# Two layers of an expert in one loop: four accumulators held open, and weight pieces fetched three steps before they are split

## The chip, the core and the metric

The kernel runs on one core of a Trainium2 chip. TensorE (PE) multiplies, VectorE (DVE), ScalarE (ACT) and GpSimd (POOL) work on tiles in on-chip memory, SyncE (SP) issues most of the transfers, ACT and POOL issue some. Each engine takes its instructions strictly in the order in which they stand, and an instruction that waits holds back all that stand behind it on that engine. The metric is the device time of one execution in microseconds (us); less is better.

## What is computed

Three stages follow each other on 4608 tokens of 512 features, in float32. The change lies in the second, so that stands here in full, and the others in a line or two:

```python
# 1: retention (8 batches, 8 heads, 576 positions, 64 features a head): x, 4608 x 512
ret = (scale * q @ k.T) * Dmat ; x = ret @ v
# 2: a layer of 8 experts; each token goes to the expert with the largest logit
expert_idx = argmax(normed(x) @ normed(expert_emb).T / tau)
for e in range(8):
    mask = expert_idx == e
    h = maximum(x[mask] @ w1[e], 0.0)          # 512 -> 1024
    out[mask] = gate_w[mask, None] * (h @ w2[e])   # 1024 -> 512
# 3: a dense layer, weights given in float64 by their bits
h = x @ w_in ; g = h * cos(h) ; y = g @ w_out  # 512 -> 2048 -> 512
```

## The kernel before

Every float32 product is done as three matmuls on operands split into a high and a low part (`mm3`, L84 to L87: high by high, high by low, low by high). The split of a weight is two instructions: ACT rounds the fetched piece to the high part (L190), POOL subtracts to get the low part (L191). `fetch_piece` (L176) issues the transfer of a piece of 128 x 1024 values on SP into one of three staging buffers (`st`), `split_piece` (L184) makes the split; `load_piece` does one right behind the other.

Stage 1 scatters each token's row to a region of its expert in a table in memory. Stage 2 takes the experts in order of their size; each expert's tokens are cut into two blocks ("halves", 16 in all, of 312 down to 272 columns by `HCS`). For a block:

- `load_half` brings the token rows (tile `nat`), `rows_to_x` turns them by twelve PE transposes (tile `xt`) and ACT and DVE split them (tile `x`, L267, L268).
- `layer1` runs over eight groups f of 128 hidden features: twelve matmuls into one bank of PSUM (tile `h`), then ACT takes relu into the high part of `hs` (L286) and DVE the low part (L287). All eight `hs` are kept.
- `layer2` runs over four groups d of 128 output features: for each, 24 matmuls over all eight `hs` into one bank (tile `y`), a DVE copy (L308), and a transfer of the result to a buffer in memory, `x2t[d]` (L309).

So all of `layer1` of a block stands ahead of its transposes for the next block, and these ahead of `layer2`. The pieces of the next expert's weights are loaded beside: the four of w1 when the expert's first block begins, the four of w2 in the second block after every other f. From the fourth block on, `decode64` turns 32 pieces of the float64 weights of stage 3 into float32, in the same staging buffers: seven instructions on ACT, DVE and POOL and a transfer back to memory (`wf`). At the first block of the first expert stands an `If` for experts with more tokens than two blocks hold; with this input its body isn't run.

Stage 3 (`load_x2`, `ffn1_mm`, `ffn2`) reads `x2t` back, 512 columns at a time and one d after the other, splits it (tile `xf`, L825, L826) and alternates the matmuls of the first layer (tile `f`) with those of the second, which go into four accumulators held open (tile `o`). It begins with six groups of `f` that go over d in the outer loop.

The order in which each engine's instructions stand is made by a scheduler from the order of the code, its dependencies and its own estimates of time; `tc.issue_after(x)` forces an instruction behind x on its engine. PSUM has eight banks, and every `bank(...)` takes a free one and waits for the readers of the last tile in it.

Of the kernel before, what the change touches and what calls it, by code (L numbers as in the profile page):

```python
# [36 lines left out]
DECODE_AT = ((0, 2, 4), (0, 2))  # L37
# [12 lines left out]
PAD = 2  # L50
PIECE_AT = ((3, 2), (3, 4), (4, 0), (5, 2), (5, 4), (6, 0))
# [3 lines left out]
def retention_moe_ffn(  # L55
# [116 lines left out]

    wcount = [0]
    wpools = {"a": wa}

    def fetch_piece(src, a, nm):  # L176
        st = stage.tile([P, 1024], F32, tag="st", name=f"st{nm}")
        nc.sync.dma_start(st.rearrange("p (a b) -> p a b", a=a) if a > 1 else st, src)
        return st
# [17 lines left out]
    def w2_src(e, i):  # L197
        return w2[ds(e, 1), :, i * P : (i + 1) * P].rearrange("o (c p) d -> p (o c) d", p=P)

    def w1_piece(e, i):  # L200
        return load_piece(w1_src(expert[e], i), 4)

    def w2_piece(e, i):
        return load_piece(w2_src(expert[e], i), 8)

    def win_piece(i):
        return load_piece(wf32[i], 1)
# [8 lines left out]
    def decode64(n):  # L216
        i, c = n // 2, n % 2
        st = stage.tile([P, 1024], F32, tag="st", name=f"sd{n}")
        if i < 8:
            src = w_in32[c * 256 : (c + 1) * 256, i * 512 : (i + 1) * 512].rearrange("(c p) f -> p c f", p=P)  # L220
            nc.sync.dma_start(st.bitcast(I32).rearrange("p (a b) -> p a b", a=2), src)
        else:
            nc.sync.dma_start(st.bitcast(I32), w_out32[(n - 16) * P : (n - 15) * P, :])
# [4 lines left out]
        tb = mp["dec"].tile([P, 512], F32, tag="tb", name=f"tb{n}")  # L228
        nc.scalar.activation(ta, hi_f, AF.Abs)
        nc.vector.scalar_tensor_tensor(hi_f, ta, TINY64, hi_f, op0=ALU.is_ge, op1=ALU.mult)  # L230
# [6 lines left out]
        nc.vector.tensor_scalar(tb.bitcast(I32), lo_w, 9, None, op0=ALU.logical_shift_right)  # L237
# [4 lines left out]
        nc.sync.dma_start(wf32[i][:, c * 512 : (c + 1) * 512], ta)  # L242
# [3 lines left out]
    def load_rows(row0, nm, pool, hc):  # L246
# [3 lines left out]
        for ins in (i1, i2):  # L250
            after_all("xs", ins)
        return t

    def copy_ids(row0, col0, hc):
        ins = nc.sync.dma_start(idl[ds(col0, hc), :], xs_d[ds(row0, hc), DM : DM + 1])
        after_all("xs", ins)

    def rows_to_x(t, nm, pool, hc):
        x = pool.tile([P, 2, NP, hc], F32R, tag="x", name=f"x_{nm}")
        for c in range(3):  # L260
            n = P if c < 2 else hc - 256
            ps = bank(f"xt{c}_{nm}")
            for d in range(NP):
                nc.tensor.transpose(ps[:, d * n : (d + 1) * n], t[:n, c, d * P : (d + 1) * P], ident[:n, :n])
            pv = ps[:, : NP * n].rearrange("p (a b) -> p a b", a=NP)
            hi = x[:, 0, :, c * P : c * P + n]
            nc.scalar.copy(hi, pv)  # L267
            nc.vector.tensor_tensor(x[:, 1, :, c * P : c * P + n], pv, hi, op=ALU.subtract)  # L268
        return x

    def layer1(x, wp, nm, hc, after=None):
        hs = []
        for f in range(FE // P):
            ps = bank(f"h{f}_{nm}")
            w = wp(f // 2)
            for c in range(NP):
                o = c * 256 + (f % 2) * P
                mm3(
                    ps[:, :hc],
                    lambda s: w[:, s, o : o + P],  # L280
                    lambda s: x[:, s, c, :],
                    c == 0,
                    c == NP - 1,
                )
            h = mp['h'].tile([P, 2, hc], F32R, tag="h", name=f"hs{f}_{nm}")
            nc.scalar.activation(h[:, 0], ps[:, :hc], AF.Relu)  # L286
            nc.vector.scalar_tensor_tensor(  # L287
                h[:, 1], ps[:, :hc], 0.0, h[:, 0], op0=ALU.max, op1=ALU.subtract
            )
            hs.append(h)  # L290
            if after is not None:
                after(f)
        return hs

    def layer2(hs, wp, nm, col, hc, after=None, queue=None):
        for d in range(NP):
            ps = bank(f"y{d}_{nm}")
            w = wp(d)
            for f in range(FE // P):
                mm3(  # L300
                    ps[:, :hc],
                    lambda s: w[:, s, f * P : (f + 1) * P],
                    lambda s: hs[f][:, s],
                    f == 0,
                    f == FE // P - 1,
                )
            y = mp["y"].tile([P, hc], F32, tag="y", name=f"y{d}_{nm}")
            nc.vector.tensor_copy(y, ps[:, :hc])  # L308
            (queue or nc.sync).dma_start(x2t[d][:, ds(col, hc)], y)  # L309
            if after is not None:  # L310
                after(d)
# [5 lines left out]
    w1p, w2p = {}, {}  # L317
# [6 lines left out]

    def load_half(i):
        e, j = halves[i]
        natt[i] = load_rows(entry(1 + j, e), f"{e}_{j}", natp[i % 3 != 1], HCS[e])
# [3 lines left out]
    with ExitStack() as actx:  # L331
# [282 lines left out]
        for i, (b, c) in enumerate(seq):  # L614
# [8 lines left out]
            if i == len(seq) - 1:  # L623
                x0 = rows_to_x(early["rows"], "0_0", xp[0], HCS[0])
# [12 lines left out]
            if fetched and fetched[0][0] <= i - 2:  # L637
                key, st = fetched.pop(0)[1:]
                with tc.issue_after(state["pool"].ins):
                    (w1p if key < 4 else w2p)[(0, key % 4)] = split_piece(st)  # L640
# [351 lines left out]
```

## Time and profile before

| | us |
|---|---|
| time, median of 3 runs | 1524.63 (1522.89 to 1530.38) |
| the profiled execution: its time, its span | 1515.07, 1511.8 |
| its mean granted TensorE clock, as a share of full speed | 0.966 |
| PE busy | 1431.9 (95% of the span) |
| DVE, POOL, ACT busy | 684.7, 571.1, 566.5 |
| first `h` matmul of the first block | at 197.3 |
| first `h` matmul behind the `If` | at 235.15 |
| first `f` matmul of stage 3 | at 716.85 |

The profile is of one execution. A view is a table of rows from it: of instructions in order of time (start, duration, engine, line, operation, tile written and tiles read, and in brackets how long the engine sat idle before and what ended that), of who waited for whom, of busy time in a stretch, or of groups of like instructions. Matmuls overlap, so the duration of one is longer than the distance from one to the next, and it is the distance that counts. The granted clock is the share of TensorE's 2.4 GHz that it was given; it has two levels, 1 and 0.5 (1.2 GHz).

### The profile page before, as it was taken

Reading aid. Unit: us, or ns where it says so; the run is one execution under the profiler, and the core shown is the slowest. Engines: PE = TensorE matmul, PEld = TensorE weight load, DVE = VectorE, ACT = ScalarE, POOL = GpSimd, SP = SyncE. Lnnn points to the kernel's source line nnn. Section 1 sums busy time; section 2 is a strip of 40 time slices with the busy share of each in tenths; the row PEclk is TensorE's granted clock in tenths of the full one; section 3 lists DMA queues with packets and bytes.
Section 4 is the critical chain, followed back from the end, with each engine's and each line's share of the span. In section 5 each row is a group of like instructions: output and inputs, shape, how many; then the busy total and the mean of one; then the engine's idle time right before and its main releaser. Section 6 shows DMA issues by size and latency. Waiting matters only on the chain.

```text
span 1511.8 us, 23820 instructions
## 1 busy us (share of the span) xinstructions
PE 1431.9 (95%) x9272; PEld 1258.1 (83%) x9272; DVE 684.7 (45%) x1344; ACT 566.5 (37%) x1016; POOL 571.1 (38%) x401
## 2 busy tenths in 40 slices
PE   8888997898999999979999999999999999999997
PEld 7777787898999989879888888888888888888885
DVE  5666751325263463552554444344444434444432
ACT  3434542323333334323543334343343434334332
POOL 2445334434545555535353232232323222232322
PEclk8989998999999999999999999999999999999998
DMA  9878545736667576665310100001010101000000
GB/s 357 302 250 275 184 138 108 174 100 166 166 176 183 155 198 160 163 142 154 100 56 29 29 28 28 1 28 28 29 28 28 29 7 33 16 29 1 28 1 28
DMA packets 110363, 156.39 MB, mean 103 GB/s; under 512 B 16503, under 2 KB 73975, under 8 KB 110247
## 3 DMA queue, kind: packets, MB, share of 16 engines
q1 hardware_dynamic: 103028, 134.34, 31.6%
q0 software_dynamic: 5760, 19.17, 3.3%
q8 instruction: 74, 1.21, 0.3%
q10 hardware_dynamic: 1458, 1.33, 0.3%
q14 instruction: 43, 0.34, 0.1%
HBM read 117.47 MB, written 37.36 MB: 102 GB/s over the span
## 4 chain that ended last, share of the span: by engine, by line
PE 61%; DMA 12%; DVE 4%; POOL 3%; issue 2%; ACT 2%; SPq 1%; POOLq 0%; ACTq 0%; DVEq 0%
PE f L86 8%; PE f L87 8%; PE f L85 8%; PE o L85 8%; PE o L87 8%; PE o L86 8%; DMA st<-in_moe_w_dram 5%; DMA wf<-ta 3%; PE y L86 2%; POOL w L191 2%; PE y L87 2%; PE y L85 2%; DMA sd<-in_moe_w_in_dram 2%; PE h L85 1%; PE h L87 1%
## 5 line engine op out<-in xcount | busy, mean ns | idle before, releaser
L857 POOL TENSOR_TENSOR g<-kk,g 128x512 fp32r<-128x512 f32 x143 | 184.8, 1293 | 511.7 <-ACT g L856 511.5
L191 POOL TENSOR_TENSOR w<-st,w 128x1024 fp32r<-128x1024 f32 x74 | 177.6, 2411 | 147.6 <-ACT w L190 137.7
L86 PE MATMUL f<-xf,w 128*128 128x512 f32 x576 | 224.2, 389 | 0.1
L86 PE MATMUL o<-w,g 128*128 128x512 f32 x576 | 224.1, 389 | 0.0
L87 PE MATMUL f<-xf,w 128*128 128x512 f32 x576 | 224.1, 389 | 0.0
L85 PE MATMUL o<-w,g 128*128 128x512 f32 x576 | 223.7, 389 | 0.2 <-DVE kk L854 0.2
L85 PE MATMUL f<-xf,w 128*128 128x512 f32 x576 | 222.5, 389 | 0.0
L87 PE MATMUL o<-w,g 128*128 128x512 f32 x576 | 219.2, 389 | 0.0
L852 ACT ACTIVATE sn<-kk 128x512 f32<-128x512 f32 x144 | 91.0, 632 | 321.3 <-DVE kk L850 320.9
L849 DVE TENSOR_SCALAR kk<-f 128x512 f32<-128x512 f32 x144 | 99.5, 691 | 231.4 <-PE f L87 225.2
L854 DVE SCALAR_TENSOR_TENSOR kk<-sn,f 128x512 f32<-128x512 f32 x144 | 99.0, 688 | 183.9 <-ACT sn L853 183.7
L85 PE MATMUL y<-hs,w 128*128 128x312 f32 (+7 forms) x512 | 164.1, 321 | 18.8 <-ACT hs L286 13.8
L86 PE MATMUL y<-hs,w 128*128 128x312 f32 (+7 forms) x512 | 163.9, 321 | 10.2 <-DVE hs L287 9.8
L87 PE MATMUL y<-hs,w 128*128 128x312 f32 (+7 forms) x512 | 160.1, 313 | 0.0
L85 PE MATMUL h<-x,w 128*128 128x312 f32 (+7 forms) x512 | 155.8, 304 | 4.4 <-DVEq L720 4.4
L87 PE MATMUL h<-x,w 128*128 128x312 f32 (+7 forms) x512 | 154.5, 302 | 0.0
L86 PE MATMUL h<-x,w 128*128 128x312 f32 (+7 forms) x512 | 154.5, 302 | 0.0
L856 ACT CAST g<-kk 128x512 fp32r<-128x512 f32 x144 | 89.4, 621 | 114.5 <-DVE kk L854 113.7
L86 PEld LDWEIGHTS f<-xf,w 128*128 128x128 f32 x576 | 108.3, 188 | 23.0 <-DVE xf L826 0.5
L85 PEld LDWEIGHTS o<-w,g 128*128 128x128 f32 x576 | 108.2, 188 | 23.0 <-DVE kk L854 0.6
L87 PEld LDWEIGHTS o<-w,g 128*128 128x128 f32 x576 | 108.2, 188 | 22.5
L85 PEld LDWEIGHTS f<-xf,w 128*128 128x128 f32 x576 | 108.0, 188 | 22.4
(156 smaller groups left out, 2337.6 us busy)
## 6 DMA issues: line engine op xcount, KB each, us to landing
st<-in_moe_w_dram SPq DMA_DIRECT2D x58, 512.0 KB, 5.2
kv<-in_kv_dram SPq DMA_DIRECT2D x36, 512.0 KB, 6.9
qk<-in_qk_dram SPq DMA_DIRECT2D x35, 512.0 KB, 5.1
xs<-x2t SPq DMA_DIRECT2D x36, 256.0 KB, 3.1
nat<-xs_d SPq DMA_DIRECT2D x16, 528.0 KB, 6.8
sd<-in_moe_w_in_dram SPq DMA_DIRECT2D x16, 512.0 KB, 5.7
wf<-ta SPq DMA_DIRECT2D x32, 256.0 KB
sd<-in_moe_w_out_dram SPq DMA_DIRECT2D x16, 512.0 KB, 7.4
```

Source lines behind the costliest of these rows:

```text
L85: keep(MM(ps, lhs(0), rhs(0), start=first, stop=False))
L86: keep(MM(ps, lhs(0), rhs(1), start=False, stop=False))
L87: keep(MM(ps, lhs(1), rhs(0), start=False, stop=last))
L191: nc.gpsimd.tensor_tensor(wt[:, 1], st, wt[:, 0], op=ALU.subtract)
L849: nc.vector.tensor_scalar(kk, ps, MAGIC, MAGIC, op0=ALU.add, op1=ALU.subtract)
L852: nc.scalar.activation(sn, kk, AF.Sin, scale=math.pi)
L854: evac = nc.vector.scalar_tensor_tensor(kk, sn, 0.5, ps, op0=ALU.subtract, op1=ALU.mult)
L856: lasti[:] = evac, nc.scalar.copy(gt[:, 0], kk)
L857: (nc.vector if (t, m) == seqf[-1] else nc.gpsimd).tensor_tensor(gt[:, 1], kk, gt[:, 0], op=ALU.subtract)
```

## The change

Stage 2 becomes one loop over 16 blocks of eight steps. Step f of a block issues twelve matmuls of `h` (`h_step`) for f, then those of `y` (`y_step`) for a group two groups back (`YLAG`), across the border of blocks: in steps 0 and 1 of a block the `y` matmuls of f 6 and 7 of the block before. `y_step` adds the product of one `hs` to four open accumulators, one bank each, three matmuls in each; at f 7 each is copied and sent off. `hs` is now five buffers where it was eleven. The transposes for the next block are cut into three and stand behind the `h` matmuls of steps 3, 4 and 5.

The pieces of w2 are cut the other way (256 hidden features by all 512 outputs, where they were 1024 by 128), w1 and w2 pieces take turns, and each is fetched in one step and split `FETCH` = 3 steps on, every second step (every step for the second expert). The split is held behind the last relu on ACT (`behind("act")`). The decoding gets staging buffers of its own (two) and begins one piece every third step from step 8; its instructions are spread over steps 3, 4 and 6 after the fetch. Every DMA of a block's result in the last block still goes by ACT, now all four behind the last `y` matmul, and the last two pieces of w_in are loaded behind that in the code.

```diff
-    def layer1(x, wp, nm, hc, after=None):
...
+    def h_step(x, w, f, nm, hc, pool):
+        ps = bank(f"h{f}_{nm}")
+        for c in range(NP):
+            o = c * 256 + (f % 2) * P
+            mm3(
...
+        h = pool.tile([P, 2, hc], F32R, tag="h", name=f"hs{f}_{nm}")
+        last["act"] = nc.scalar.activation(h[:, 0], ps[:, :hc], AF.Relu)
+        last["dve"] = nc.vector.scalar_tensor_tensor(
+            h[:, 1], ps[:, :hc], 0.0, h[:, 0], op0=ALU.max, op1=ALU.subtract
+        )
+        return h
+
+    def y_step(acc, h, w, f, nm, hc, col, pool, queue=None):
+        if f == 0:
+            acc[:] = [bank(f"y{d}_{nm}") for d in range(NP)]
         for d in range(NP):
...
+            o = (f % 2) * DM + d * P
+            mm3(
+                acc[d][:, :hc],
+                lambda s: w[:, s, o : o + P],
+                lambda s: h[:, s],
+                f == 0,
+                f == FE // P - 1,
+            )
+            if f == FE // P - 1:
+                y = pool.tile([P, hc], F32, tag="y", name=f"y{d}_{nm}")
+                nc.vector.tensor_copy(y, acc[d][:, :hc])
+                (queue or nc.sync).dma_start(x2t[d][:, ds(col(), hc)], y)
...
+    def split_expert(e, p):
+        with behind("act"):
+            wp[(e, p)] = split_piece(sts.pop((e, p)))
...
+        for e in range(1, E):
+            for p in range(8):
+                at = SPLIT_0[p] if e == 1 else (e - 1) * 16 + 2 * p + 2
+                if e > 1 or p > 2:
+                    steps[at - FETCH].append(lambda e=e, p=p: fetch_expert(e, p))
+                steps[at].append(lambda e=e, p=p: split_expert(e, p))
...
+            for f in range(FE // P):
+                if f == 0 and i + 2 < len(halves):
                     load_half(i + 2)
...
+                block_h(i, f)
+                if i + 1 < len(halves) and f > 2 and f < 6:
...
+                    rows_chunk(xs[i + 1], natt[i + 1], f - 3, f"{e1}_{j1}", HCS[e1])
+                if len(pendy) > YLAG:
+                    block_y()
+                for job in steps[i * 8 + f]:
+                    job()
+        cols[len(halves) - 1] = col_last
+        for _ in range(YLAG):
+            block_y(nc.scalar)
+        for n in (6, 7):
+            winp[n] = load_piece(wf32[n], 1)
+        woutp[0] = wout_piece(0)
```

How the instructions stand on PE at one border, that of the first block of the third expert (names carry expert, block and a running number: `hs_2_0` belongs to expert 2, block 0). Before, the last `h`, the transposes and the first `y`:

```order
L86 MATMUL h_2_0_4938<-x_0_4590,w_4106 128x310
L87 MATMUL h_2_0_4938<-x_0_4590,w_4106 128x310
L264 MATMUL xt_2_1_4955<-ident,nat_1_4411 128x128 x4
L264 MATMUL xt_2_1_4962<-ident,nat_1_4411 128x128 x4
L264 MATMUL xt_2_1_4969<-ident,nat_1_4411 128x54 x4
L85 MATMUL y_2_0_4995<-hs_2_0_4797,w_4462 128x310
L86 MATMUL y_2_0_4995<-hs_2_0_4797,w_4462 128x310
L87 MATMUL y_2_0_4995<-hs_2_0_4797,w_4462 128x310
L85 MATMUL y_2_0_4995<-hs_2_0_4827,w_4462 128x310
```

Now, from the last accumulators of the block before (`y_1_1`) over one `h` group (twelve matmuls in all, three shown) to the first of the new block's accumulators:

```order
L92 MATMUL y_1_1_4538<-hs_1_1_4740,w_4129 128x330
L90 MATMUL y_1_1_4539<-hs_1_1_4740,w_4129 128x330
L91 MATMUL y_1_1_4539<-hs_1_1_4740,w_4129 128x330
L92 MATMUL y_1_1_4539<-hs_1_1_4740,w_4129 128x330
L90 MATMUL h_2_0_4875<-x_0_4578,w_4378 128x310
L91 MATMUL h_2_0_4875<-x_0_4578,w_4378 128x310
L92 MATMUL h_2_0_4875<-x_0_4578,w_4378 128x310
...
L90 MATMUL y_2_0_4891<-hs_2_0_4801,w_4296 128x310
L91 MATMUL y_2_0_4891<-hs_2_0_4801,w_4296 128x310
L92 MATMUL y_2_0_4891<-hs_2_0_4801,w_4296 128x310
L90 MATMUL y_2_0_4892<-hs_2_0_4801,w_4296 128x310
```

The first `y` of a block now stands two `h` groups behind the `h` whose `hs` it reads, where it stood behind all eight; four banks change hands here within 24 matmuls.

On ACT in the middle of the stage, before: relu (L286), weight splits (L190), casts of `x` (L267) and the decoding's first instruction (L229) of one block's end.

```order
L286 ACTIVATE hs_1_1_4566<-h_1_1_4553 128x330
L286 ACTIVATE hs_1_1_4582<-h_1_1_4569 128x330
L190 CAST w_4587<-st_4585 128x1024
L267 CAST x_0_4590<-xt_2_0_4591 128x4x128
L267 CAST x_0_4590<-xt_2_0_4598 128x4x128
L267 CAST x_0_4590<-xt_2_0_4605 128x4x54
L190 CAST w_4754<-st_4752 128x1024
L190 CAST w_4759<-st_4757 128x1024
L190 CAST w_4764<-st_4762 128x1024
L229 ACTIVATE ta_4802<-sd_4800 128x512
L190 CAST w_4769<-st_4767 128x1024
```

Now, the same engine in the same block:

```order
L298 ACTIVATE hs_1_1_4620<-h_1_1_4607 128x330
L196 CAST w_4642<-st_5_4518 128x1024
L277 CAST x_0_4578<-xt_2_0_4623 128x4x128
L298 ACTIVATE hs_1_1_4658<-h_1_1_4645 128x330
L234 ACTIVATE ta_4683<-sd_4560 128x512
L277 CAST x_0_4578<-xt_2_0_4661 128x4x54
L298 ACTIVATE hs_1_1_4702<-h_1_1_4689 128x330
L196 CAST w_4717<-st_6_4598 128x1024
L243 ACTIVATE tb_4684<-tb_4684 128x512
L298 ACTIVATE hs_1_1_4740<-h_1_1_4727 128x330
L298 ACTIVATE hs_2_0_4801<-h_2_0_4788 128x310
L196 CAST w_4816<-st_7_4680 128x1024
```

The splits that stood in a row between two blocks stand one at a time, each behind a relu.

On ACT at the end of the stage, before: the last block's results go off (`x2t`, in d order) between splits of stage 3's weights, and the casts `xf` of what is read back follow each:

```order
L309 DMA x2t_70<-y_7_1_8821 128x272
L190 CAST w_8859<-st_8857 128x1024
...
L309 DMA x2t_71<-y_7_1_8854 128x272
L190 CAST w_8892<-st_8890 128x1024
...
L309 DMA x2t_72<-y_7_1_8887 128x272
L825 CAST xf_8951<-xs_0_8952 128x512
L825 CAST xf_8951<-xs_1_8956 128x512
L190 CAST w_8970<-st_8968 128x1024
...
L309 DMA x2t_73<-y_7_1_8920 128x272
L825 CAST xf_8951<-xs_2_8960 128x512
```

Now:

```order
L196 CAST w_8767<-st_8765 128x1024
...
L319 DMA x2t_70<-y_7_1_8739 128x272
...
L319 DMA x2t_71<-y_7_1_8745 128x272
...
L319 DMA x2t_72<-y_7_1_8751 128x272
...
L319 DMA x2t_73<-y_7_1_8757 128x272
L196 CAST w_8772<-st_8770 128x1024
L196 CAST w_8822<-st_8820 128x1024
L196 CAST w_8827<-st_8825 128x1024
L866 CAST xf_8803<-xs_0_8804 128x512
L866 CAST xf_8803<-xs_1_8808 128x512
```

The four results leave together, behind the last `y` matmul of all, and three splits stand between them and the first cast of stage 3's input.

## Rows read from the trace of the kernel before

**Rows 1.** Stretches: us, busy PE, PEld, DVE, ACT, POOL, PEclk, DMA share, GB/s.

```profile
230.40:235.15 4.75, 0.31 (x4) 0.08 (x2) 1.98 (x4) 2.86 (x5) 4.75 (x3) 0.87 0.52 136
235.15:716.85 481.70, 444.77 (x3049) 433.18 (x3050) 202.96 (x382) 161.72 (x289) 235.63 (x127) 0.94 0.63 157
716.85:1487.90 771.05, 770.75 (x3400) 637.78 (x3399) 333.53 (x480) 301.76 (x484) 233.18 (x182) 1.00 0.09 28
```

**Rows 2.** PE's waits from 235.15 to 716.85: total us, times, longest us.

```profile
PE y L85 <- ACT hs L286: 13.8, 6, 5.6
PE y L86 <- DVE hs L287: 9.8, 17, 2.4
PE xt L264 <- DVE hs L287: 7.9, 2, 5.9
PE y L85 <- DVE hs L287: 4.7, 2, 4.1
```

**Rows 3.** PE and DVE in order of time, a border of blocks: start, us, [idle before].

```profile
359.72 1.42 PE L264 MATMUL xt<-ident,nat 128*128 128x128 f32 x12
365.28 0.62 PE L85 MATMUL y<-hs,w 128*128 128x310 f32 x1 [4.15 <-DVE hs L287]
...
364.41 0.43 DVE L237 TENSOR_SCALAR tb<-sd 128x512 int32<-128x512 int32 x1 [5.47 <-DMA sd<-in_moe_w_in_dram]
364.75 0.47 DVE L287 SCALAR_TENSOR_TENSOR hs<-h,hs 128x310 fp32r<-128x310 f32 x1
```

**Rows 4.** Groups, same stretch: line, count, busy us, mean ns, idle before.

```profile
L190 ACT CAST w<-st 128x1024 fp32r<-128x1024 f32 x62 | 64.8, 1045 | 92.9 <-DMA st<-in_moe_w_dram 63.0 <-PE y L87 22.6 <-DMA st<-wf 5.6
L287 DVE SCALAR_TENSOR_TENSOR hs<-h,hs 128x330 fp32r<-128x330 f32 (+7 forms) x120 | 54.7, 463 | 88.5 <-ACT hs L286 88.5
L286 ACT ACTIVATE hs<-h 128x330 fp32r<-128x330 f32 (+7 forms) x120 | 47.5, 415 | 98.3 <-PE h L87 96.4 <-SPq L720 1.9
```

**Rows 5.** PE at half clock after a wait: first and last of 21 matmuls.

```profile
259.37 0.46 PE L86 MATMUL y<-hs,w 128*128 128x312 f32 x1
...
264.57 0.34 PE L85 MATMUL y<-hs,w 128*128 128x312 f32 x1
```

**Rows 6.** PE at full clock: the first and last of 51 matmuls.

```profile
244.06 0.30 PE L87 MATMUL h<-x,w 128*128 128x312 f32 x1
...
251.25 0.31 PE L86 MATMUL h<-x,w 128*128 128x312 f32 x1
```

**Rows 7.** The staging tile's transfers, issue to landing.

```profile
DMA to landing us min/median/max: 3.8/5.5/14.9
```

**Rows 8.** PE in stage 3, from an accumulator to the next `f`.

```profile
902.49 0.39 PE L87 MATMUL o<-w,g 128*128 128x512 f32 x1
902.71 0.39 PE L85 MATMUL f<-xf,w 128*128 128x512 f32 x1
```

**Rows 9.** DVE in order of time, before the `If` and at the stage's end.

```profile
234.39 0.47 DVE L308 COPY y<-y 128x312 f32<-128x312 f32 x1
...
717.04 0.44 DVE L308 COPY y<-y 128x272 f32<-128x272 f32 x1 [2.56 <-PE y L87]
```

**Rows 10.** ACT at the stage's end: sending `y`, splitting weights, casting `xf`.

```profile
709.26 0.36 ACTq L309 DMA_DIRECT2D x2t<-y  x1
...
719.50 0.34 ACTq L309 DMA_DIRECT2D x2t<-y  x1
719.76 1.04 ACT L190 CAST w<-st 128x1024 fp32r<-128x1024 f32 x1
...
726.29 0.62 ACT L825 CAST xf<-xs 128x512 fp32r<-128x512 f32 x1 [2.94 <-DMA xs<-x2t]
```

**Rows 11.** SP there: reading `x2t` back.

```profile
711.45 0.38 SPq L821 DMA_DIRECT2D xs<-x2t  x1
...
723.44 1.76 SPq L821 DMA_DIRECT2D xs<-x2t  x4
```

**Rows 12.** Transfers: KB each, median us from issue to landing.

```profile
xs<-x2t SPq DMA_DIRECT2D x36, 256.0 KB, 3.1
```

More of the change, by code (lines that the diff above doesn't have):

```diff
@@ L256, in copy_ids, with new_x, rows_chunk @@
         after_all("xs", ins)
+        last["sp"] = ins
+    def new_x(nm, pool, hc):
+        return pool.tile([P, 2, NP, hc], F32R, tag="x", name=f"x_{nm}")
+    def rows_chunk(x, t, c, nm, hc):
+        n = P if c < 2 else hc - 256
+        ps = bank(f"xt{c}_{nm}")
+        for d in range(NP):
+            nc.tensor.transpose(ps[:, d * n : (d + 1) * n], t[:n, c, d * P : (d + 1) * P], ident[:n, :n])
+        pv = ps[:, : NP * n].rearrange("p (a b) -> p a b", a=NP)
+        hi = x[:, 0, :, c * P : c * P + n]
+        nc.scalar.copy(hi, pv)
+        nc.vector.tensor_tensor(x[:, 1, :, c * P : c * P + n], pv, hi, op=ALU.subtract)
@@ L258, in rows_to_x @@
     def rows_to_x(t, nm, pool, hc):
-        x = pool.tile([P, 2, NP, hc], F32R, tag="x", name=f"x_{nm}")
+        x = new_x(nm, pool, hc)
         for c in range(3):
[L261 to L268, printed above, removed]
@@ L295, in layer2 @@
-    def layer2(hs, wp, nm, col, hc, after=None, queue=None):
-        for d in range(NP):
[L297 to L311, printed above, removed]
+            rows_chunk(x, t, c, nm, hc)
@@ new lines, in retention_moe_ffn, with win_fetch, win_split @@
+        steps = [[] for _ in range(len(halves) * 8)]
+        for e in range(1, E):
[4 more added lines that the diff above has]
+                steps[at].append(lambda e=e, p=p: split_expert(e, p))
+        def win_fetch(n):
+            sts[n] = fetch_piece(wf32[n], 1, f"in{n}")
+        def win_split(n):
+            with behind("act"):
+                winp[n] = split_piece(sts.pop(n))
@@ new lines, in retention_moe_ffn, with dec_fetch, dec_run @@
+        for n, at in enumerate(SPLIT_7):
+            steps[(E - 1) * 16 + at - FETCH].append(lambda n=n: win_fetch(n))
+            steps[(E - 1) * 16 + at].append(lambda n=n: win_split(n))
+        sd, dec = {}, {}
+        def dec_fetch(n):
+            sd[n] = decode_fetch(n)
+        def dec_run(n):
+            if n in sd:
+                dec[n] = decode64(n, sd.pop(n))
+            with behind("act"), behind("dve"):
+                next(dec[n])
+        for n in range(32):
+            at = DECODE_FROM + DECODE_EVERY * n
+            steps[at].append(lambda n=n: dec_fetch(n))
+            for k in (0, 1, 3):
+                steps[at + FETCH + k].append(lambda n=n: dec_run(n))
```

228 lines of the change are left out of this document (102 added, 126 removed).

## The prediction

> **What bounds the kernel now.** I read the busy time by stretches first, since a share of the whole span mixes stages with different limits. Stage 3 (716.85 to 1487.90) has PE busy for 770.75 of 771.05 us at a granted clock of 1.00: nothing is to be had there, and the change leaves its loop as it was. Blocks 2 to 16 of stage 2 (235.15 to 716.85) last 481.70 us; PE is busy for 444.77 of them at a mean clock of 0.94, and DVE, ACT and POOL for 203, 162 and 236, none near half [rows 1]. So PE is the bound there too, but it stands idle 36.9 us and is slowed besides. That slowing is worth about (1 − 0.94) × 481.7 = 28.9 us, together 65.8.
>
> A second way to the same size, by count: full clock shows (251.25 − 244.06) / 50 = 0.1438 us from one matmul to the next at 312 columns [rows 6]. The 15 blocks hold 15 × 192 = 2880 matmuls of on average 297.6 columns (from `HCS`), so 0.137 each: 395 us, and 14 groups of twelve transposes at 1.42 us [rows 3], 20 us. 481.7 − 415 = 67. I take 66.
>
> Next, PE's list of waits: the largest of that stretch are all on `hs`, the output of the first layer, the instructions that read a bank of `h` and write `hs`, whether `y` or the transposes `xt` wait for the result or for the bank: 13.8, 9.8, 7.9 and 4.7 us, 36.2 of the 36.9 [rows 2]. An `hs` costs 0.415 us on ACT and 0.463 on DVE [rows 4]; waits of 5.6 us are not its own price. What delays it shows at one border in order of time: PE has done its transposes at 361 and then idles until 365.28, because the DVE half of `hs` starts at 364.75, because the decoding instruction ahead of it on DVE sat 5.47 us waiting for its piece from memory [rows 3]. ACT does the same with weight splits: they wait 63.0 us for `st` transfers, and a relu behind such a split waits too [rows 4]. After such a wait PE runs at the lower level: 21 matmuls are (264.57 − 259.37) / 20 = 0.260 us apart where 0.144 is the pace [rows 5, 6], so one wait costs another 20 × 0.116 = 2.3 us.
>
> **The change, part by part.**
>
> *The wait for `hs`.* Today nothing but twelve transposes stands between the last `h` of a block and the first `y`; that `y` begins a bank, which an `hs` instruction must have read, and 21 matmuls on it wants the last `hs`. With the lag of two, the matmuls that read an `hs` stand behind four groups of twelve, 48 × 0.137 = 6.6 us after its `h`. The relu and its low part take 0.415 + 0.463 = 0.9 [rows 4], so 5.7 us of delay on ACT and DVE are covered. Removed: all 36.2 us, if the delays stay below that.
>
> *The pieces.* ACT's split now stands three steps behind its fetch: a step is 24 matmuls, 3.3 us, so the lead is 9.9 us. A transfer lands in 5.5 us at the median and 14.9 at worst [rows 7]. The median has 4.4 us to spare; the worst holds ACT for 5.0 us, within the 5.7 that `hs` can bear. PE waits only if a piece is over 15.6 us late, which no transfer here was. The work itself fits: relu, splits and casts, with DVE's and POOL's shares, were 203, 162 and 236 us over 15 blocks [rows 1], so 13.5, 10.8 and 15.7 a block against 27.7 us of PE (415 / 15). The three staging buffers hold a piece for about four steps and one is asked for every two, so two suffice; only the second expert asks for one a step, and there the queue is paced by transfer and split (5.5 + 1.0 us [rows 4, 7] and POOL's part of 2.4, my estimate, over three buffers: 3 us), just below a step.
>
> *What stays.* Some delays will add up (decode, casts of `x` and a split in one step). I bound the rest of the loss from both sides: 0 if all waits are covered, 10 if a quarter of the 36.9 stays. I take 4. Gain here: 66 − 4 = 62.
>
> *The `If`.* From the last `y` matmul before it (230.40) to the first `h` behind it (235.15) are 4.75 us [rows 1]. The last copy of `y` starts only at 234.39 [rows 9], 4 us late, since two `y` buffers wait for their way to memory and weight work stands among them. Now there are four buffers, and no split stands there: four copies of 0.47 us and little else, about 2 us. Gain 2.7; the ends are 0 (the wait stays) and 4.4 (all goes).
>
> *The end of the stage, a new wait.* Today the last block finishes its `y` one d at a time; d 0 leaves at 709.26, d 3 at 719.50 [rows 10], and stage 3 began at 716.85 on what was there. Now all four accumulators end within the last twelve matmuls, and PE has no work but what needs the results back. From there: the copy, 0.44 us [rows 9]; ACT's issue and the write, bounded by 709.26 to 711.45, 2.2 us (SP's read of it starts), and 719.50 to 723.44, 3.9 [rows 10, 11]; the read, 3.1 [rows 12]; the cast, 0.62 [rows 10]. The first accumulator ends about 1.1 us before the last matmul. Sum: 0.44 + 3.0 + 3.1 + 0.62 − 1.1 = 6.1; three weight splits stand ahead of the cast on ACT, and the last of them waits for a transfer issued at that moment (5.5), about as long. I take 6.4, between 4.5 and 9. PE then starts at the lower level, 2.3 more as above: −8.7. Behind the cast are queued the casts of the other three d, which come in its train.
>
> **Sum.** 62 + 2.7 − 8.7 = 56.0. The profiled execution took 1515.07; 1515.07 − 56.0 = 1459.1. The median of the runs shown, 1524.63, is 9.6 above the profiled one. I expect the same of the runs after: 1468.7, say 1468.
>
> **Rivals.**
>
> *The pieces still come late.* Fetches stand on SP among row loads, results and the decoding's transfers, each of which may wait for its buffer; a blocked SP eats the lead of 9.9 us. For it: the longest landing, 14.9 [rows 7], and traffic that now shares fewer microseconds. Against: the median, and a DMA share of 0.63 [rows 1]. If half the loss stays, 31 us less is gained: 1500.
>
> *Slower: the banks take the place of `hs`.* Four accumulators change hands at each of 15 borders. The next block's third and fourth need the banks of the old ones, which come free by copies on DVE; about 2.3 us of matmuls (17) cover these. If a decoding instruction with its piece still on the way stands ahead of the copies on DVE, as at 364.41 for 5.47 us [rows 3], PE waits 5.47 − 2.3 = 3.2 and loses 2.3 more to the clock. At every border and with one more such wait per block on ACT's side that is 15 × 5.5 = 83 in place of 66: 1515 + 17 − 2.7 + 8.7 = 1538 profiled, 1548. It decides against the change from (66 + 2.7 − 8.7) / 15 = 4.0 us a border. Against it: the decoding is asked for only every third step and three steps ahead, so it meets a border at few blocks.
>
> *The clock falls without a long wait.* In stage 3 PE goes from four open accumulators `o` to `f` and back with 0.22 us from the one to the other (902.49 to 902.71) [rows 8], at a clock of 1.00 throughout [rows 1]; if the changed stage 2 ran otherwise and lost 2.3 us at each border, 15 × 2.3 = 35 would go: 1503. The Trainium skill ("TensorE: Matmul & The Clock Gate", section "A second HAM failure mode: psum-queue depth-cycling") speaks for this rival: where PSUM banks are cycled in each iteration, PE idles briefly between groups often enough for the clock to go up and down. By that rule stage 3 of this kernel should show it, and its rows do not.
>
> *Nothing changes.* The four waits go, and splits, casts or bank copies fill the same time: 1515 + 8.7 − 2.7 with the old loss, 1521 profiled, up to 1530. For it, PE's idle time has several releasers already. Against: no engine is half busy.
>
> **Chances and range.** A measurement of this kernel tells about 0.5% from no change, 7.6 us. The forecast, 0.74, of itself 1455 to 1486 (the residue of 0 to 10, the `If` of 0 to 4.4, the stage's end of 4.5 to 9, and some 5 for the runs' distance from the profiled one). Late pieces 0.11; the clock alone 0.03; the banks 0.07; nothing 0.05. The first three are faster by over 0.5%, 0.88; nothing is the same, 0.05; the banks are slower, 0.07. The range from 1453 to 1505 takes in the first three and leaves some 0.17 out.
>
> **What would show it.** In the changed profile: PE's waits for `hs` between the `If` and stage 3 are gone or below 5 us in sum, with the granted clock of that stretch at 0.99 or more and its length near 420. ACT may still wait for `st`, without PE behind it. The gap at the `If` is near 2 us. Before the first `f` PE idles 5 to 9 us, ended by ACT's `xf`. Stage 3 from there takes 771 as before. The forecast is wrong if PE waits at borders for a DVE copy, if waits for `hs` or for `w` stay at 20 us or more, or if the clock of the stretch is still 0.94.

## The result, and the profile after

1487.44 us median (1483.83 to 1489.93, four runs) against 1525.47 for the kernel before: ratio 0.9745, 95% interval 0.9713 to 0.9777. Forecast were 1468 and a range of 1453 to 1505. So the sign and the range held, and the gain of 38 us is two thirds of the 56 forecast. The profiled execution after took 1487.71, at the median of its runs, where that of before lay 9.6 to 10.4 below its own; between the two profiles, on which the terms can be checked, the spans fell by 26.0 us only (1511.8 to 1485.8). Of the 56 us that the terms add up to, the profiles show less than half; that the medians fell by some 11 us more than the profiled times is explained by no term, and so the median's nearness to its forecast (19 us, where the terms miss by 30) is in part luck; without it the time would still be inside the range.

The profile after by stretches, which answer to those of [rows 1]: the `If`, blocks 2 to 16, the stage's end, stage 3. Columns: us, then busy us of PE, PEld, DVE, ACT, POOL with their counts, granted clock, DMA share, GB/s.

```profile
232.40:241.86 9.46, 0.02 (x2) 0.03 (x1) 1.32 (x4) 0.00 (x0) 0.00 (x0) 0.73 0.65 114
241.86:680.04 438.18, 424.29 (x3048) 420.72 (x3048) 227.65 (x381) 161.68 (x290) 236.81 (x128) 0.97 0.66 173
680.04:688.54 8.50, 0.29 (x4) 0.08 (x2) 1.09 (x4) 3.64 (x5) 6.45 (x3) 0.73 0.90 264
688.54:1461.70 773.16, 772.99 (x3398) 639.48 (x3399) 333.65 (x478) 299.74 (x482) 229.40 (x181) 1.00 0.08 26
```

Term by term against the profile before:

| | before | after | gained | forecast |
|---|---|---|---|---|
| from the first `h` behind the `If` to the last `y` (before: to the first `f`, which then came at the last `y`) | 481.70 | 438.18 | 43.5 | 62 |
| gap at the `If` | 4.75 | 9.46 | −4.7 | 2.7 |
| from the last `y` to the first `f`, and stage 3 behind it | 771.05 | 781.66 | −10.6 | −8.7 |
| from the first `h` (197.30, 197.50) to the `If` | 33.1 | 34.9 | −1.8 | 0 |
| sum | | | 26.4 | 56.0 |

PE's waits after, from first `h` to first `f` (total us, times, longest), which answer to [rows 2]:

```profile
PE h L90 <- PEq L758: 9.4, 1, 9.4
PE f L90 <- ACT xf L866: 8.2, 1, 8.2
PE y L91 <- DVE hs L299: 6.2, 1, 6.2
PE xt L274 <- DVE x L278: 5.6, 1, 5.6
PE rk L545 <- DVE ohb L535: 2.7, 1, 2.7
PE y L90 <- ACT hs L298: 2.0, 1, 2.0
```

No row has a count above 1. The waits at each border are gone; what is left are six single ones. In one stretch that holds ten borders, the same window of both kernels (before, then after), all of the loss is gone:

```profile
290.00:590.00 300.00, 282.29 (x1925) 274.51 (x1924) 134.83 (x253) 103.66 (x187) 149.60 (x82) 0.95 0.62 161
...
290.00:590.00 300.00, 300.00 (x2171) 297.74 (x2170) 181.86 (x302) 120.38 (x218) 176.15 (x100) 1.00 0.74 194
```

The count of PE's instructions in 300 us is 13% higher, at a clock of 1.00. In the same window ACT and DVE stood waiting for fetched pieces (weights `st`, pieces to be decoded `sd`) for 91.8 us before, in five rows, of which the three largest are shown, and for 2.2 after:

```profile
ACT w L190 <- DMA st<-in_moe_w_dram: 30.7, 12, 5.7
ACT ta L229 <- DMA sd<-in_moe_w_in_dram: 22.5, 5, 8.1
DVE tb L237 <- DMA sd<-in_moe_w_in_dram: 29.5, 9, 6.2
...
DVE tb L233 <- DMA sd<-in_moe_w_out_dram: 2.2, 1, 2.2
```

How late an `hs` is follows from this. From the end of its twelfth `h` matmul to the end of its low part, the traces of this window have up to 12.6 us before, with 24 of 73 beyond 6.6 us, the time of 48 matmuls; after, the longest of 85 is 4.2.

The loss that stays in blocks 2 to 16, 438.2 − 415 = 23 us, is three of the waits above (2.0, 5.6 and 6.2, 14 with what surrounds them) and four stretches at half clock behind them and the `If`: 19 + 14 + 12 + 25 = 70 matmuls x 0.12 = 8.4.

**The wait of 6.2** is seen on DVE (start, us, instruction, idle before):

```profile
593.25 0.44 DVE L299 SCALAR_TENSOR_TENSOR hs<-h,hs 128x278 fp32r<-128x278 f32 x1
605.82 0.18 DVE L848 CAST idx<-idx_f 128x36 int32<-128x36 f32 x1 [12.14 <-DMA idx_f<-idl]
605.91 0.44 DVE L299 SCALAR_TENSOR_TENSOR hs<-h,hs 128x278 fp32r<-128x278 f32 x1
...
606.41 0.60 PE L91 MATMUL y<-hs,w 128*128 128x278 f32 x1 [6.17 <-DVE hs L299]
```

The cast of the row numbers for stage 3's output stands last in the code of the stage in both kernels, and in both the scheduler put it ahead of low parts of `hs`. Before, it came in the last block and held DVE for 9.2 us with six low parts behind it; PE lost 0.76 us:

```profile
705.01 0.18 DVE L807 CAST idx<-idx_f 128x36 int32<-128x36 f32 x1 [9.18 <-DMA idx_f<-idl]
705.11 2.17 DVE L287 SCALAR_TENSOR_TENSOR hs<-h,hs 128x272 fp32r<-128x272 f32 x6
...
705.60 0.40 PE L86 MATMUL y<-hs,w 128*128 128x272 f32 x1 [0.76 <-DVE hs L287]
```

There all eight `h` groups stood ahead of the first `y`, so low parts in the middle of them could be late at little cost. Now each has no more than the two groups of the lag. The copies of row numbers on which the cast depends now stand with the row loads, two blocks ahead, and the cast came some 75 us ahead of the stage's end, where it was 12 us.

**The gap at the `If`** is PE's own branch, the jump over the body that isn't run: 10.24 us, where it was 3.77 (name, count, min/median/max ns, when; before, then after):

```profile
L720 PEldq COMPARE_BRANCH  x1: 3768/3768/3768, 228.6 to 228.6; - x1
...
L758 PEldq COMPARE_BRANCH  x1: 10241/10241/10241, 230.7 to 230.7; - x1
```

What SP issues there, after:

```profile
227.11 0.94 SPq L263 DMA_DIRECT2D idl<-xs_d  x1
230.32 0.40 SPq L255 DMA_DIRECT2D nat<-xs_d  x1
230.98 0.30 SPq L256 DMA_DIRECT2D nat<-xs_d  x1
236.34 0.94 SPq L263 DMA_DIRECT2D idl<-xs_d  x1
238.67 1.88 SPq L184 DMA_DIRECT2D st<-in_moe_w_dram  x3
```

And before, where the first copy of row numbers (`idl`, 312 elements of 4 bytes) stood behind the `If`:

```profile
218.78 0.26 SPq L249 DMA_DIRECT2D nat<-xs_d  x1
219.30 13.23 SPq L178 DMA_DIRECT2D st<-in_moe_w_dram  x4
240.12 1.06 SPq L255 DMA_DIRECT2D idl<-xs_d  x1
```

The second expert's first piece was asked for 22.0 us after the first `h`, now 41.2 us. More than half of this delay of 19.2 us is SP's own waiting. All copies of row numbers write one table (`idl`), and a copy is issued only when the one before it has landed; the pieces stand behind on SP. SP's waits from 213 to 242 (total us, times, longest):

```profile
SPq L263 <- DMA idl<-xs_d: 10.2, 2, 5.5
```

PE's waits of 2.0 and 5.6 us (253 to 271) go back to ACT, which stood at the splits of these pieces for 5.7 and 9.7 us.

**The stage's end** runs as described: copy, write, read, cast, in order of time.

```profile
679.60 1.48 DVE L318 COPY y<-y 128x272 f32<-128x272 f32 x4 [2.87 <-PE y L92]
680.07 2.83 ACTq L319 DMA_DIRECT2D x2t<-y  x4
684.59 3.12 SPq L862 DMA_DIRECT2D xs<-x2t  x4
687.84 1.16 ACT L866 CAST xf<-xs 128x512 fp32r<-128x512 f32 x2
```

From issue of the write to that of the read are 4.5 us, beyond the 2.2 to 3.9 that bounded it. The first accumulator's last matmul stood 0.74 us ahead of the last of all (679.28, 680.02), where the forecast had 1.1.

### The profile page after: what moved, and what is told of

It reads as the page before. It is cut to its first block, busy times and chain, and to the rows that moved or that the text cites. A ratio compares the mean times of both kernels' runs of the same rounds, so it can differ in the third digit from the quotient of the medians.

```text
span 1485.8 us, 23793 instructions
## 1 busy us (share of the span) xinstructions
PE 1414.7 (95%) x9272; PEld 1248.2 (84%) x9272; DVE 711.5 (48%) x1344; ACT 565.0 (38%) x1016; POOL 569.7 (38%) x401
## 4 chain that ended last, share of the span: by engine, by line
PE 77%; DMA 2%; issue 1%; POOL 1%; ACT 1%; DVE 1%; SPq 0%; POOLq 0%; ACTq 0%; DVEq 0%
PE f L90 9%; PE f L91 9%; PE f L92 9%; PE o L90 8%; PE o L92 8%; PE o L91 8%; PE y L90 4%; PE y L91 4%; PE y L92 4%; PE h L90 4%; PE h L91 4%; PE h L92 4%; PE xt L274 1%; DMA st<-in_moe_w_dram 1%; DMA idl<-xs_d 1%
## 5 line engine op out<-in xcount | busy, mean ns | idle before, releaser
L197 POOL TENSOR_TENSOR w<-st,w 128x1024 fp32r<-128x1024 f32 x68 | 166.1, 2446 | 126.9 <-ACT w L196 67.9
L91 PE MATMUL y<-hs,w 128*128 128x312 f32 (+7 forms) x512 | 156.0, 305 | 6.3 <-DVE hs L299 6.2
L90 PE MATMUL y<-hs,w 128*128 128x312 f32 (+7 forms) x512 | 158.7, 311 | 2.0 <-ACT hs L298 2.0
L92 PE MATMUL y<-hs,w 128*128 128x312 f32 (+7 forms) x512 | 155.2, 303 | 0.0
L298 ACT ACTIVATE hs<-h 128x312 fp32r<-128x312 f32 (+7 forms) x128 | 53.8, 420 | 251.8 <-PE h L92 249.0
L299 DVE SCALAR_TENSOR_TENSOR hs<-h,hs 128x312 fp32r<-128x312 f32 (+7 forms) x128 | 59.5, 465 | 164.0 <-ACT hs L298 163.4
```

What stands on the lines that cost most here:

```text
L90: keep(MM(ps, lhs(0), rhs(0), start=first, stop=False))
L91: keep(MM(ps, lhs(0), rhs(1), start=False, stop=False))
L92: keep(MM(ps, lhs(1), rhs(0), start=False, stop=last))
L197: nc.gpsimd.tensor_tensor(wt[:, 1], st, wt[:, 0], op=ALU.subtract)
L298: last["act"] = nc.scalar.activation(h[:, 0], ps[:, :hc], AF.Relu)
L299: last["dve"] = nc.vector.scalar_tensor_tensor(h[:, 1], ps[:, :hc], 0.0, h[:, 0], op0=ALU.max, op1=ALU.subtract)
```

## The experiments

Stage 1 is the same code in all, but its length differs between executions: the first `h` stands at 197.3 to 216.3 in the profiles. So beside the ratio I give the time from first `h` to last `y` of the profiled execution, which that does not touch. Before: 519.4; after: 482.5, and 474.7 in a second profile (the last run). So two profiles of one kernel differ by 7.8 us in this measure: a difference of that size between two runs shows nothing by itself, and what a run says then is read from the wait in question.

**One cast moved (e1_idx_late).**

```diff
-        nc.vector.tensor_copy(idx, idx_f)
+        with behind("copy"):          # the last copy of y
+            nc.vector.tensor_copy(idx, idx_f)
```

> The changed kernel with one instruction moved on DVE: the cast of the row numbers (idx), which waited 12.1 us for its transfer at 593.7 to 605.8 with a low part of hs behind it, is held behind the last copy of y. Theory (one instruction in the wrong place): PE's wait of 6.2 us at 606.4 goes, and with it 25 matmuls at half clock (25 x 0.12 = 3.0), so 9.3 us off the profiled 1487.7: about 1478.4, the stretch from the If to the last y 438.2 -> about 429. Rival (the transfers of that moment are late for everybody, the cast only showed it): another instruction takes over the wait at the same border, under 3 us gained.

0.9745 (0.9713 to 0.9777); first `h` to last `y` 470.6, no wait for `hs` behind 282. The wait and the slow matmuls went and no wait took their place. Against the 474.7 that is 4 us, not the 9 expected: in the runs of this kernel that keep the cast, DVE waits 8.1 to 12.1 us there and PE 1.9 to 7.2; the profile shown above had the longest on DVE. By the ratio alone the effect can't be told.

**Row loads behind the `If` (e2_rows_later).** `load_half(2)` moves from before the `If` to the first step behind it.

> The changed kernel with the row loads of the third block (680 KB, and 312 row numbers) issued behind the If instead of just before it. Theory (PE's branch takes 10.24 us because the code that it jumps to is fetched while the rows are): the branch comes down towards the 3.8 us that it took in the kernel before, the gap at the If from 9.46 to about 4; and SP reaches the first fetches of the second expert's weights some 10 us earlier, so that the two waits at 253 and 264 (2.0 and 5.6 us, with 26 slow matmuls 3.1 more) shrink too: 5 to 16 us off 1487.7. Rival 1 (the jump is long whatever the transfers do): the gap stays at 9 to 10, and only the waits behind it change. Rival 2 (the rows now come late): a new wait of the third block's transposes for nat, 2 us or more, at about 255.

0.9785 (0.9745 to 0.9825); 476.1. The branch took 11.06 us: it isn't the third block's row loads. The first theory fell; rival 1 was closer (PE waited 10.3 us there). In this run too copies of row numbers stood ahead of the branch and of the pieces.

**No `If` (e3_no_if).**

> The changed kernel without the If and its body (experts with more tokens than two blocks hold are left out; this input has none). Theory (the gap of 9.46 us is the branch of PE alone: its operands are there by 233): the gap falls to about 1, the 19 slow matmuls behind it may go too (2.3): 8 to 11 us off 1487.7. Rival (PE would have waited for x, weights or rows anyway): the gap stays above 5 and the gain under 4. For the second expert's pieces both leave it open: PE arrives earlier, so their waits at 253 and 264 may grow by what is gained here.

0.9730 (0.9699 to 0.9761); 468.0. The gap at the `If` is gone, but 11.9 us are waited for `hs` at 267, behind ACT's sending of the first block's results (261.7 to 267.0), which waited in turn until rows, a copy of row numbers and pieces had landed, 12.4 us at the first of the four. By the measure 7 us were gained against the 474.7, no more than two profiles of one kernel differ; the rest of what was expected came back as this wait. So branch and transfers are late side by side; whether one thing holds up both, this run doesn't show.

**The end by accumulators (e4_end_by_d).** The last four `hs` are kept and taken d by d, and the last three weight pieces are loaded behind the first casts in the code:

```diff
+        for d in range(NP):
+            for i, f, h in fin:       # the last four hs
+                mm3(acc[d][:, :hc], ..., False, f == FE // P - 1)
+            ... copy, send off
```

> The changed kernel with the last four hs of the last block held back and taken one accumulator after the other, so that the first accumulator ends 36 matmuls before the last, not 9; the last three weight pieces are loaded behind the first casts in the code. Theory (the end of the stage costs one copy, write, read and cast behind the first accumulator): the wait for xf falls from 8.2 us by 27 x 0.125 = 3.4 to about 4.8, the 2.1 us of slow clock behind it stay: about 1484. Rival (the three splits ahead of the cast on ACT set the end): the wait falls by more than 5, below 3 us. Rival (the transfers are slow because four writes and a weight piece share the queues): the chain is as long from each accumulator on, the wait stays above 7.

0.9734 (0.9703 to 0.9764); the wait for `xf` 7.2 us, a gain of 1 and not 3.4. The order of the code wasn't kept: the scheduler took the accumulators' matmuls in turns again, the first ended some 15 matmuls before the last. The run says nothing on the theory; it is tried again below.

**Copies of row numbers later (e5_ids_late).**

```diff
-        copy_ids(row, cols[i], HCS[e])
+        if i > 3:
+            copy_ids(row, cols[i], HCS[e])
+        # blocks 0 to 3: issued in steps 18, 20, 22 and 24
```

> The changed kernel with the copies of the row numbers (idl) of the first four blocks, some 312 elements of 4 bytes each, issued in steps 18 to 24 instead of beside the row loads, ahead of the If and of the second expert's first weights. Theory (what is issued behind such a copy is slow: in the traces 20 to 50 packets of rows or weights in 2 us for some 8 us, single ones of 3 to 7 us; the If's code and the second expert's pieces stand behind them): rows and pieces land sooner, PE's branch takes under 5 us, the waits behind the If (9.4, 2.0, 5.6 us) come to under 6 in sum; first h to last y falls from 482 (476 in the run without the row loads there) to 462 to 467. Rival 1 (the rows of 2112 bytes are slow by themselves): branch and waits stay within 3 us of what they were. Rival 2 (the copies only move their harm): new waits of 3 us or more between steps 18 and 30.

0.9721 (0.9685 to 0.9757); 468.0, just short of the 462 to 467 expected. The branch takes 3.6 us, the gap is 3.1, the first piece is asked for 23.9 us after the first `h`, and the waits behind the `If` are gone. What the transfers do shows in their rate, in 40 slices of 0.4 us: 226 to 242 after, and 228 to 244 of this run, where the same rows are asked for at 231.7:

```profile
GB/s 37 111 100 227 386 222 94 3 0 0 0 0 20 48 74 37 0 5 21 37 90 42 32 63 42 21 53 111 37 169 299 415 364 224 101 102 229 193 26 31
...
GB/s 264 0 0 0 0 132 153 312 391 401 211 85 132 327 338 364 179 75 98 155 375 311 244 260 242 303 231 242 262 343 361 364 154 84 74 56 90 49 218 209
```

Behind a copy of row numbers (issued at 227.11, in the third slice of the first row) the rows of 230.3 trickle at 0 to 111 GB/s for some 7 us; without it they and the pieces behind them run mostly at 150 to 400. SP's 10.2 us of waiting for the copies ahead of the `If` are gone here too. The run takes away both, the slow transfers and SP's waits, and doesn't say what each is worth. Rival 2 holds too: at 312 and 317 are two new waits of 2.8 and 3.0 us, where the four copies now stand every second step among pieces and decoding. The second, `y` for a DVE copy of `y`, is the wait for a bank that the prediction had as a rival.

**That part alone, in the kernel before (e6_before_ids_early).** The copies of blocks 0 to 2 beside their row loads, ahead of the pieces and the `If`; the rest is the kernel before.

> The kernel before with this part of the change alone: the copies of the row numbers of the first three blocks stand beside the row loads, ahead of the second expert's weights and the If, not behind the first layer. Theory (these copies cost the changed kernel what it lost at the If): the gap at the If grows from 4.75 to 8 or more, and the second expert's first pieces land 8 us or more later: slower by 4 to 15 us. Rival (the longer branch comes from the new code of stage 2): no difference over 3 us.

1.0027 (1.0007 to 1.0046); first `h` to last `y` 527.9 in place of 519.4, the gap at the `If` 14.4 us, the first piece 37.4 us after the first `h` (22.0). The direction and the gap are as the theory has them; the time of the whole is at the low end of the 4 to 15 us expected, 3.8 in the medians. SP waited 10.6 us for the copies here too. The branch itself took only 4.28 us, and what PE waited for was DVE: its casts of `x` and a copy of `y` (260.8 to 262.8) had waited 14.4 us for ACT, which stood 13.0 us at the sending of a result, until a copy of row numbers landed, and 10.4 us at a split whose piece came late. So a slow branch isn't the rule behind such copies; in the profiles of the changed kernel and its variants that keep them ahead of it, it took 6.1 to 11.1 us, in those without them (and before) 3.4 to 3.8.

**No lead in the code (e7_fetch0), a lag of one (e8_lag1), both (e10_lag1_fetch0).** One constant each: `FETCH = 0`; `YLAG = 1` (a loop of the first block that it also set stays at two).

> The changed kernel with FETCH = 0: pieces, and those to be decoded, are fetched in the step in which they are split. Theory (hs bears 5.7 us of delay; a piece lands 5.7 us after its fetch, behind a relu of the same step): most waits stay covered, ACT waits 3 to 5 us at each split, PE loses under 25 us more than with FETCH = 3, in a few waits for hs behind long landings. Rival A (the lead is what matters): ACT stands 1 us or more beyond the slack at most of the 100 pieces, PE loses 40 us or more and the clock falls again to 0.95 or less. Rival B (the lead is worth nothing): the time is within 4 us.

0.9778 (0.9750 to 0.9806); 474.3: rival B, no difference that can be told.

> The changed kernel with YLAG = 1: y stands one group behind h, so 24 matmuls (3.3 us) and not 48 cover relu and low part, 2.4 us to spare where there were 5.7. Theory: with pieces three steps ahead ACT and DVE rarely stand for more than a decoding instruction or a split (0.4 to 2.5 us): some waits of under 1 us, 3 to 15 us more in all. Rival A (the lag of two carries the gain): waits for hs in most blocks, 25 us or more. Rival B: no difference beyond 3 us, the lag could be one.

0.9787 (0.9758 to 0.9815); 477.0: 2 us more, rival B.

> The changed kernel with YLAG = 1 and FETCH = 0 together, each of which alone moved nothing that could be told. Theory (each covers for the other: a piece that lands 5.7 us after its fetch is beyond the 2.4 us that a lag of one leaves): PE waits for hs in most blocks, the stretch from first h to last y grows from 475 to 495 or more, the clock of it falls below 0.96. Rival (that both layers share each step is enough, PE always has twelve matmuls of the other layer): within 8 us of the run with the lag alone.

0.9786 (0.9745 to 0.9827); 479.1: the rival again. The same window as above, of this run:

```profile
290.00:590.00 300.00, 300.00 (x2157) 297.90 (x2156) 180.82 (x300) 118.02 (x212) 179.19 (x102) 1.00 0.73 194
```

Why the lead in the code is worth nothing shows in the time from a piece's issue on SP to its split on ACT, over the some 40 pieces issued in 290 to 590: median 17.5 us after, 16.5 with `FETCH = 0`, 16.5 with both, and 9.1 before. SP runs ahead of PE until no buffer is free, whatever step the code names: its largest wait in this window is for POOL to free a staging buffer, 58.4 us after and 65.0 with `FETCH = 0`. So these runs didn't take the lead away, and what they show is narrower than meant: that `FETCH` doesn't make it. What differs from before is that the pieces have the three staging buffers to themselves, and the decoding two of its own.

The lag does what the sum said of it, but is rarely called on. The one long wait on DVE, for the row numbers, measures its cover: with a lag of two, 12.1 us on DVE cost PE 6.2, and 8.3 cost it 2.1; with a lag of one, 10.3 cost 7.2. That is 5.9 and 6.2 us covered with two (the forecast had 5.7), 3.1 with one (2.4). The two ends with two and with one (the second profile of the changed kernel, then the run with lag one and no lead):

```profile
PE y L91 <- DVE hs L299: 2.1, 1, 2.1
...
PE y L91 <- DVE hs L299: 7.2, 1, 7.2
```

**The fetches alone, in the kernel before (e9_before_spread).** Layers one after the other; pieces fetched three steps of twelve before a split that stands behind a relu:

```diff
+            steps[max(12, at - FETCH)].append(fetch)
+            steps[at].append(split)      # behind the last relu on ACT
```

> The kernel before, its two layers one after the other as they were, with the fetches alone taken from the change: pieces and those to be decoded are fetched three steps ahead of their split, and the splits stand behind a relu, one every second step. Theory (what goes in step carries the gain, the lead does not: without the lead the changed kernel lost nothing that could be told): waits for hs at the borders stay in sum above 20 us of the 36, 1 to 2 us at nearly each, since relu, low part and a split or decoding instruction have only twelve transposes to hide behind; 0 to 25 us faster than before. Rival (the late pieces alone made the waits): under 10 us of waits for hs are left, and it is faster by 35 us or more.

1.0117 (1.0074 to 1.0160): 1.2% slower, which neither foresaw. Waits for `hs`:

```profile
PE y L85 <- DVE hs L299: 26.9, 7, 6.8
PE y L86 <- DVE hs L299: 10.9, 12, 3.8
PE y L85 <- ACT hs L298: 4.5, 3, 3.3
...
PE xt L276 <- DVE hs L299: 2.0, 4, 0.8
```

44.3 in sum, more than before. But the lead from issue to split fell to a median of 4.6 us, while pieces and decoding still shared three buffers, and DVE waited 139.6 us for pieces to decode in 290 to 675 (80.6 and 59.0; 53.4 before, 2.2 after). So this run doesn't show what a real lead alone would give. It shows what late transfers do to the old order: they go through to PE.

**Three repairs (e11_best), and the changed kernel beside it (e12_after_again).** Copies at steps 44, 60, 76 and 92; the cast at the end; the last four `hs` by accumulators, with the order kept (and, as in e4, the last three weight pieces loaded behind the first casts):

```diff
+                mm3(..., f == FE // P - 1, tc.keep_in_program_order)
```

> The changed kernel with three repairs: the copies of the row numbers of the first four blocks at steps 44, 60, 76 and 92, where nothing is short; the cast of the row numbers behind the last copy of y; the last four hs taken one accumulator after the other, in a fixed order this time (in the run that tried it the scheduler had mixed them again, so that the first accumulator ended 14 matmuls before the last). Theory: gap at the If about 3 us, no wait of 3 us or more from there to the last y, first h to last y 455 to 460 (468 in the run with late copies less 8.5 for the two waits that they moved and 4 to 6 for the cast); the wait for xf 4 to 6 us in place of 8.3. Against the kernel before 0.958 to 0.965. Rival (the repairs only move the waits): above 465 and a ratio above 0.970.

> The changed kernel again, beside the repaired one on the same chip. Every theory: ratio to the kernel before 0.971 to 0.978, first h to last y 474 to 483, gap at the If above 8 us, a wait for hs behind the cast of the row numbers of 2 to 6 us, 8 to 9 us ahead of the first f.

0.9661 (0.9625 to 0.9697) and 0.9768 (0.9736 to 0.9801) against the same runs of before: 1477.63 us beside 1494.32; the intervals don't meet. First `h` to last `y` 457.4 beside 474.7. The changed kernel came out as expected, but for PE's wait at the `If`, 7.6 us, where above 8 was expected. The repaired kernel's stretch from the `If` to the last `y`, and PE's waits from 225 on:

```profile
253.99:673.79 419.80, 417.28 (x3048) 414.01 (x3048) 228.17 (x381) 161.95 (x290) 237.59 (x128) 1.00 0.67 177
```

```profile
PE f L90 <- ACT xf L885: 3.5, 1, 3.5
PE h L90 <- PEq L767: 2.9, 1, 2.9
PE h L90 <- DVE hs L299: 2.4, 1, 2.4
```

419.8 us is what the forecast had for this stretch (415 and a rest of 4). The wait for `xf` is 3.5, a little below the 4 to 6 expected. The wait of 2.4 at 556 is new: ACT's first decoding instruction waited 7.6 us for a write to memory that was issued at 535.74, beside the row loads and the copy of row numbers of its own block. The ratio is 0.001 above what was expected. The repairs give some 17 us, and the copies account for it: from the first `h` to that of the third block, where they act, are 63.0 us, beside 81.0.

## Why the prediction was right, and where it was short

- *PE is the bound of stage 2 and loses 66 us at the borders, by waits for `hs` and the clock behind them*: right. From 290 to 590 the loss is nothing, at a clock of 1.00.
- *The lag covers 5.7 us*: right as a size, 5.9 and 6.2 measured. That this cover is why the waits go is not shown: with a lag of one, 3 us of cover, they stay away as well, and an `hs` is now 4.2 us late at most, where 12.6 was seen. With the delays of before, a lag of two would not have covered the 24 of 73 that were more than 6.6 us late (an estimate from these counts). What the traces show to be gone is the lateness itself: ACT and DVE hardly wait for fetched pieces any more (2.2 us from 290 to 590, before 91.8).
- *The lead of three steps*: the lead is there, 17.5 us, but not from `FETCH`; SP ran ahead. The buffers of their own are the likely source; not tried alone.
- *What stays, 0 to 10, I take 4*: this is the step that failed. 23 us stayed. The steady blocks have none of it: it is the cast that the scheduler put ahead of an `hs` (6.2 us of waiting and 25 slow matmuls, in this profile; the old order bore the same cast for 0.8), and the second expert's pieces, for which I had worked out the pace of three buffers ("just below a step") but not when the first is asked for. `load_half` now calls `copy_ids`, a line of the diff that I gave no cost: SP waits 10.2 us between the copies, and what is issued behind them is slow.
- *The `If`, gain 2.7, ends 0 and 4.4*: wrong in sign, −4.7, from the same line. I had cost what waits on DVE, and not PE's branch, whose 3.8 us in the trace of before had looked like a part of DVE's wait.
- *The end of the stage, 6.4 and 2.3*: 8.5 and 2.1. The write took 4.5 us from issue to read where I took 3.0, and the first accumulator ended 0.7 us ahead where I took 1.1.
- *Median and profile*: the profile before was 10 us quicker than its median, the one after was not; part of the distance that I carried over may be stage 1's, whose end moved between 197 and 216 us in fourteen profiles.
- *The rivals*: banks and the clock by itself did not show in the changed kernel (in e5 one wait for a bank did, 3.0 us). PE was busy for 325.40 of 325.40 us from 274.5 to 599.9, with four accumulators open and banks of `h` changing at each border. The rule of the Trainium skill ("TensorE: Matmul & The Clock Gate", section "A second HAM failure mode: psum-queue depth-cycling"), by which the clock goes up and down where banks are cycled, didn't apply here: the clock was 1.00 from 290 to 590.

Open: whether the order of the two layers or the buffers carry the 43 us. The run meant to part them lost its lead; the kernel before with two more staging buffers would do it, and was not tried. Why transfers behind the 4-byte copies are slow is not shown either, only that they are, and their share and that of SP's waits between the copies were not parted.

## What to carry to other kernels

Where an in-order engine sits idle behind a transfer, look at what is queued behind it; work of another layer between producer and consumer covers such a wait, here 6 us with a lag of two; better is that the wait doesn't arise, for which buffers of their own for unrelated streams are the likely means here (not tried alone). In a large rewrite, cost the small lines that come along: a few copies of some hundred 4-byte elements, each waiting for the one before, were issued ahead of urgent transfers, and a cast waits for such copies, which the old order bore and the new one doesn't. Mending these two, and the stage's end, gave some 17 us. A constant in the code that says when a transfer is issued isn't the lead: measure from issue to use.

## What the runs showed of the hardware

- Behind a transfer of 312 elements of 4 bytes, transfers of rows and weights ran at 0 to 111 GB/s for about 7 us, where they else had mostly 150 to 400; with these copies moved away the slow stretch was gone (e5). Where three such copies into one table stood on SP, the second and third were issued only when the one before had landed, 10.2 us of waiting in all (10.6 in e6).
- A branch of PE over the body of an `If` that isn't run took 3.4 to 3.8 us, and 6.1 to 11.1 in the changed kernel and its variants with such transfers in front of it; in the kernel before with them in front (e6) it took 4.3. In all thirteen profiles that have the `If` the branch ended 0.8 to 1.5 us after a fetch of 16 KB of instructions. Where it was long, this fetch either started late, 6.0 to 8.7 us behind the branch (7.9 after, e2, e4, e12), or took 4.3 to 6.3 us (e1, e7, e8, e10); elsewhere it started 1.0 to 1.5 us behind it and took 0.9 to 1.5.
